# Gated mix of linear and local attention on one core: 14 instead of 9 matmuls on zeros at the start, and GpSimd's sums of phi(k) placed three at a time behind attention masks

## The chip, the cores and the metric

The kernel runs on one core of a Trainium2 chip. The metric is the device time of one execution in microseconds (us); lower is better. The kernel before took 491.21 us, the median of three runs (489.88, 491.21 and 491.37).

## The reference

For one sequence of 2048 positions x 1024 features, bf16, with 32 heads of 32, two attentions are computed on the same input `A_x` and mixed by a gate for each position:

```python
g = sigmoid((x * gate_w).sum(-1, keepdims=True))
# A: linear attention
phi = lambda t: where(t > 0, t + 1, exp(t)) + 1e-6
pq, pk = phi(q), phi(k)
kv = einsum("bhsd,bhse->bhde", pk, v)
z = einsum("bhsd->bhd", pk)
o = einsum("bhqd,bhde->bhqe", pq, kv) / (einsum("bhqd,bhd->bhq", pq, z)[..., None] + 1e-6)
a = o @ wo_A
# B: softmax over the 8 keys at distances 0, 2, ..., 14
b = softmax(q . k_gathered * scale) @ v_gathered @ wo_B
out = g * a + (1 - g) * b
```

Each of A and B has its own `wqkv` and `wo`. The change touches `z`, the sum of phi(k) over all positions, and the start of the program.

## The kernel before

**How the program is ordered.** The function `plan` records every operation with an engine, a cost, what it reads and writes, and a priority (by default the order of recording). A list scheduler (`Prog.schedule`, L121) turns this into one fixed order for each engine, and `Prog.emit` (L203) writes it out with semaphore waits. Each engine executes its own queue in order. `Prog.op` takes `after=`, a list of operations that the new one must wait for beside its data. Evictions from PSUM (`move`, L1367) are recorded for "any" of ScalarE and VectorE, and the scheduler picks one.

**The stages on TensorE (PE).**

1. At L1377 a loop of `WARM` (L1242, 9) matmuls on a tile of zeros, `warm`, runs ahead of all data. They write PSUM bank 7 and nobody reads it.
2. v of B (L1383): for blocks of four x tiles and two halves of the weight, 8 matmuls of 128x512 a group. The x tiles come by transposing DMAs from the queue of SyncE (SP in the profile) (`load_x`, L1311), the first weight half in four parts, two of them from ScalarE's queue. The first group (tile 0) is recorded in four steps of two matmuls, each waiting for its part of the weight. The results go to HBM (`vB_hbm`).
3. The gate, then k and q of B (L1502), 8 + 8 column blocks for each of the two halves of positions (even and odd).
4. phi(k) of A (L1546): 16 tiles x 2 halves, each 8 matmuls, then `phi` (L1347): an exponential on ScalarE, two VectorE operations, into `pkS`, all 16 tiles of which stay in SBUF.
5. x^T phi(k) (L1602, the matmuls L1610): 8 chunks x 2 halves, 16 matmuls each, then `state` (L1584) for kv.
6. phi(q) of A, the scaling by the denominators (`scaled`, L1648, which reads `zb`), and the output matmuls (L1678).

**The attention blocks of B.** `fill` (L1431) records one block: scores on PE (L1444), an exponential of all of them on ScalarE (`E`, L1450), a multiplication by a 0/1 mask on VectorE (L1453, the "mask"), and, three slots later, the products with the values on PE (`values`, L1456, matmuls L1463 and L1469), whose sums go through a logarithm and an exponential on ScalarE (L1478, L1479) and a product on VectorE (L1480). Scores and values share PSUM banks 4 to 7. There are 18 blocks; `slot` (L1488) spreads them among the matmul groups of stages 3 to 5.

**The sums.** z is made on GpSimd (POOL in the profile): a copy of tile 0 of `pkS` to the fp32 tile `zacc`, then 15 additions of a tile of 128x1024 (L1571 to L1576). The loop stands behind the one of stage 4, and the copy waits (`after=[o]`) for the last matmul group of phi(k). Behind chunks 5 and 6 of stage 5 `z_spread` (L1558) splits one half of `zacc` into two bf16 tiles (a cast L1560 into the tile `warm`, a subtraction L1561), multiplies both by ones on PE (L1566, the "z pair") to spread the sum to all partitions, and moves the result to `zb`.

Of the kernel before, what the change touches and what calls it, by code (L numbers as in the profile page):

```python
# [7 lines left out]
ALU = mybir.AluOpType  # L8
# [1103 lines left out]
def build_kernel(nc, A_x, A_wqkv, A_wo, B_x, B_wqkv, B_wo, gate_w, out):  # L1112
    del B_x
    S = A_x.shape[1]
    NT = S // 128
# [72 lines left out]
    pkS = SB([128, NT, 1024], BF16, "pk", at=ws[1].lo)  # L1188
# [15 lines left out]
    zacc = SB([128, 1024], F32, "zacc")  # L1204
# [34 lines left out]
    FILL = 0.2  # L1239
    PVLAG = 3  # L1240
    SUMS_AT = 2
    WARM = 9  # L1242
    PASSES = 6
    mm = lambda n: max(n / 2400.0, 0.0267) + 0.0025
    act = lambda n: 0.19 + n / 1200.0
# [2 lines left out]
    def plan(seen):  # L1248

        P = Prog(nc, nc.alloc_semaphore)  # L1250
# [27 lines left out]
        for i, (n, offs) in enumerate(KINDS):  # L1278
            for h, o in enumerate(offs):
                m = mtmp[h]  # L1280
# [102 lines left out]
        for t, half in [(4 * b + i, half) for b in range(NT // 4) for half in range(2) for i in range(4)]:  # L1383
# [5 lines left out]
            for d in range(0, 8, step):  # L1389
                o = group(bank, xs, w, [xr, ws[0].part((d, d + step), (half * 512, half * 512 + 512))], d, d + step)  # L1390
            move(vt[:, :], bank.ap, 512, bank, vt.all())
            P.op("sp", lambda e, t=t, vt=vt, half=half: e.dma_start(vB_hbm[t * 128:(t + 1) * 128, half * 512:half * 512 + 512], vt[:, :]), 0.6, reads=[vt.all()],
                 writes=[hb(t * 128, (t + 1) * 128, half)], chan="vst%d" % vs, lat=0.5, prio=5)
# [32 lines left out]
        main = Pool(banks[0:4])  # L1426
        todo = []
        later = []
        slot_n = [0]

        def fill(e_, qs, nq, offs):  # L1431
            t0 = e_ * HS
            k0 = [qs + nq * h - offs[h] for h in range(2)]
            m = msk[KINDS.index((nq, offs))]
            vt, vslot = vr.next()
            for h in range(2):
                P.op("sp", lambda e, h=h: e.dma_start(vt[64 * h:64 * h + 64, :], vB_hbm[t0 + k0[h]:t0 + k0[h] + 64, :]), 0.4,
                     reads=[hb(t0 + k0[h], t0 + k0[h] + 64, i) for i in range(2)], writes=[vt.all()], chan="v%d_%d" % (vslot, h), lat=0.5)

            def s_fn(e):  # L1440
                for c in range(8):
                    for h in range(2):
                        for j in range(4):
                            last = e.matmul(SO[j].ap(c * nq, (c + 1) * nq)[64 * h:64 * h + 64, :], kT[32 * j:32 * j + 32, c, t0 + k0[h]:t0 + k0[h] + 64],  # L1444
                                            qT[32 * j:32 * j + 32, c, t0 + qs + h * nq:t0 + qs + (h + 1) * nq], start=True, stop=True, tile_position=(32 * j, 64 * h))
                return last
            P.op("pe", s_fn, 0.65, mode="r", reads=[kT.part((0, 8), (t0 + k0[0], t0 + k0[1] + 64)), qT.part((0, 8), (t0 + qs, t0 + qs + 2 * nq))],
                 writes=[s.iv for s in SO], name="S")
            E, _ = Er.next()
            P.op("act", lambda e: e.activation(E[:, 0:32 * nq].rearrange("p (j q) -> p j q", j=4), ps[:, 4:8, 0:8 * nq], ACT.Exp), act(32 * nq),  # L1450
                 reads=[s.iv for s in SO], writes=[E.all()])
            ev = lambda: E[:, 0:32 * nq].rearrange("p (g q) -> p g q", g=16)
            P.op("dve", lambda e: e.tensor_tensor(ev(), ev(), m[:, :, :].rearrange("p r q -> p (r q)")[:, None, :].to_broadcast([128, 16, 2 * nq]), ALU.mult),  # L1453
                 0.15 + 32 * nq / 1920.0, reads=[E.all(), m.all()], writes=[E.all()])

            def values():  # L1456

                def each(e):
                    for c in range(8):
                        for j in range(4):  # L1460
                            for h in range(2):
                                hd = 4 * c + j
                                last = e.matmul(SO[h].ap(c * nq, (c + 1) * nq)[32 * j:32 * j + 32, :], vt[64 * h:64 * h + 64, hd * 32:hd * 32 + 32],  # L1463
                                         E[64 * h:64 * h + 64, (8 * j + c) * nq:(8 * j + c + 1) * nq],
                                         start=True, stop=True, tile_position=(64 * h, 32 * j))
                        if c == SUMS_AT:
                            for j in range(4):
                                for h in range(2):
                                    e.matmul(SO[2 + h].ap(0, 8 * nq)[32 * j:32 * j + 32, :], ones[64 * h:64 * h + 64, 0:32],  # L1469
                                             E[64 * h:64 * h + 64, 8 * j * nq:8 * (j + 1) * nq],  # L1470
                                             start=True, stop=True, tile_position=(64 * h, 32 * j))
                    return last
                bi = [s.iv for s in SO]
                P.op("pe", each, 0.66, mode="c", reads=[vt.all(), ones.all(), E.all()], writes=bi, name="PV")
                for g in range(2):
                    L, _ = Lr.next()
                    pb = lambda o, g=g: ps[:, 4 + 2 * o:6 + 2 * o, 4 * g * nq:4 * (g + 1) * nq]
                    P.op("act", lambda e, L=L, pb=pb: e.activation(L[:, :, 0:4 * nq], pb(1), ACT.Ln), act(8 * nq), reads=[SO[2].iv, SO[3].iv], writes=[L.all()])  # L1478
                    P.op("act", lambda e, L=L: e.activation(L[:, :, 0:4 * nq], L[:, :, 0:4 * nq], ACT.Exp, scale=-1.0), act(8 * nq), reads=[L.all()], writes=[L.all()])  # L1479
                    P.op("dve", lambda e, L=L, pb=pb, g=g: e.tensor_tensor(  # L1480
                        qT[:, 4 * g:4 * g + 4, t0 + qs:t0 + qs + 2 * nq].rearrange("p c (h q) -> p h c q", h=2),
                        pb(0).rearrange("p h (c q) -> p h c q", c=4), L[:, :, 0:4 * nq].rearrange("p h (c q) -> p h c q", c=4), ALU.mult), dps(8 * nq),
                        reads=[SO[0].iv, SO[1].iv, L.all()], writes=[qT.part((4 * g, 4 * g + 4), (t0 + qs, t0 + qs + 2 * nq))])
            after(PVLAG, values)
# [12 lines left out]
        def after(n, f, cols=False):  # L1497
            later.append((slot_n[0] + n, f, cols))
            later.sort(key=lambda x: x[0])
# [68 lines left out]
            P.op("pe", fn, 2 * mm(512), reads=[ones.all()] + [z.all() for z in zh], writes=[bank.iv], name="z")  # L1568
            move(zb[:, c], bank.ap, 512, bank, zb.part((hf * 512, (hf + 1) * 512)))

        for t in range(NT):  # L1571
            src = pkS.part((t, t + 1), (0, 1024))
            if t == 0:
                P.op("pool", lambda e: e.tensor_copy(zacc[:, :], pkS[:, 0, :]), 2.0, reads=[src], writes=[zacc.all()], after=[o])
            else:
                P.op("pool", lambda e, t=t: e.tensor_tensor(zacc[:, :], zacc[:, :], pkS[:, t, :], ALU.add), 2.2, reads=[src, zacc.all()], writes=[zacc.all()])  # L1576

        main = Pool(banks[0:3])
        sb = banks[3]
        sb.take = len(takes)  # L1580
# [3 lines left out]
        def state(c):  # L1584
            def fn(e):
                for i in range(8):
                    for j in range(4):
                        h = 4 * i + j
                        last = e.matmul(sb.ap()[32 * j:32 * j + 32, i * 32:i * 32 + 32], ws[0][:, c, h * 32:(h + 1) * 32], mT[:, c, h * 32:(h + 1) * 32],  # L1589
                                        start=False, stop=(c == 7), tile_position=(0, 32 * j), skip_group_check=True)  # L1590
                return last
            P.op("pe", fn, 0.22, mode="c", reads=[ws[0].part((c, c + 1), (0, 1024)), mT.part((c, c + 1), (0, 1024))], writes=[sb.iv], name="kv")
# [3 lines left out]
        def late_w():  # L1596
            if wait_w[0] and not todo:
                wait_w[0] = False
                load_w(5, 0, Ao, 0, 52)
                load_w(5, 1, Ao, 512, 53)  # L1600

        for c in range(8):  # L1602
            tl = xns[c // 2]
            cs = (c % 2) * 128
            for r in range(2):
                bank = main.next()
                for t0 in (0, NT // 2):
                    def fn(e, bank=bank, t0=t0, tl=tl, cs=cs, r=r):
                        for t in range(t0, t0 + NT // 2):
                            last = e.matmul(bank.ap(), tl[:, t, cs:cs + 128], pkS[:, t, r * 512:(r + 1) * 512], start=(t == 0), stop=(t == NT - 1))  # L1610
                        return last
                    P.op("pe", fn, NT // 2 * mm(512), reads=[tl.part((t0, t0 + NT // 2), (cs, cs + 128)), pkS.part((t0, t0 + NT // 2), (r * 512, (r + 1) * 512))], writes=[bank.iv])
                    if t0:
                        move(mT[:, c, r * 512:(r + 1) * 512], bank.ap, 512, bank, mT.part((c, c + 1), (r * 512, (r + 1) * 512)))
                    slot(FILL)
                    late_w()
            after(3, lambda c=c: state(c))
            if c in (5, 6):
                z_spread(c - 5)
            if c % 2 == 1 and len(xns) < 4:  # L1620
                xns.append(load_xn(len(xns)))
# [113 lines left out]
    P, flag_op = best[:2]  # L1735
# [61 lines left out]
```

## Time and profile before

| | |
|---|---|
| median of three runs | 491.21 us (489.88 to 491.37) |
| the profiled execution: its own time, its span | 491.46 us, 489.6 us |
| PE busy | 476.8 us, 97% |
| VectorE (DVE), ScalarE (ACT), GpSimd (POOL) busy | 277.6, 147.7, 44.2 us |
| phi(k) of A ends, stage 5 begins on PE | about 248.5 us |
| the sums on GpSimd (L1574, L1576) | 248.5 to 285.2 us |
| the attention masks L1453 | 18, from 132.4 to 312.1 us |

The profile is of one execution. Times in it are microseconds from the start of the span; the execution's own time is 1.86 us more than its span. A row of the timeline has the start, the duration, the engine, the line of the kernel, the operation, the tile written and the tiles read, the count of merged instructions, and in brackets how long the engine had been idle and what ended that. PEld is PE's weight load, which runs beside the matmuls. A row of the waits says who waited for whom: total us, times, longest. A row of one line has the shortest, median and longest duration in ns. A row of the DMA issues ends with the us from issue to landing. A row of the table of stretches has the busy us and count of PE, PEld, DVE, ACT and POOL, then the granted clock, the DMA share and GB/s.

### The profile page before, as it was taken

What the parts mean: (1) busy time and instruction counts of PE and PEld (TensorE: products, weight loads), DVE (VectorE), ACT (ScalarE), POOL (GpSimd) and SP (SyncE); (2) the same over time, 40 slices, a digit from 0 to 9 for tenths busy, and PEclk for the clock granted to TensorE, in tenths of its full rate; (3) what the DMA queues carried; (4) which work ended last, traced back from release to release, by engine and by line L of the source; (5) the groups of instructions that cost most, each with busy time, mean ns of one, the idle gap of its engine ahead of it and who ended that gap; (6) DMA issues with size and microseconds to landing.
All of it is one profiled execution on the core that took longest, in us unless ns stands there. A gap on an engine that the chain in (4) does not pass through costs nothing.

```text
span 489.6 us, 10831 instructions
## 1 busy us (share of the span) xinstructions
PE 476.8 (97%) x4815; PEld 226.8 (46%) x4878; DVE 277.6 (57%) x457; ACT 147.7 (30%) x229; POOL 44.2 (9%) x43
## 2 busy tenths in 40 slices
PE   8999999999999999999999999999999999999997
PEld 2444444444444444444445455444444444444444
DVE  2121235556577778776652323379987777777622
ACT  1211111111333335666644454545222100011000
POOL 3000000000000000000069941000000000000000
PEclk9999999999999999999999999999999999999999
DMA  8999996000000032303003340251224211123111
GB/s 212 230 190 279 355 308 168 0 1 0 1 25 23 24 108 66 36 23 120 23 25 110 120 121 3 90 172 23 64 66 107 44 43 44 44 57 73 44 44 48
DMA packets 72496, 43.27 MB, mean 88 GB/s; under 512 B 39157, under 2 KB 68214, under 8 KB 72442
## 3 DMA queue, kind: packets, MB, share of 16 engines
q1 hardware_dynamic: 71898, 41.98, 32.2%
q8 instruction: 40, 0.66, 0.6%
q10 hardware_dynamic: 544, 0.52, 0.4%
q14 instruction: 14, 0.11, 0.1%
HBM read 25.70 MB, written 8.40 MB: 70 GB/s over the span
## 4 chain that ended last, share of the span: by engine, by line
PE 96%; issue 2%; DMA 1%; DVE 1%; ACT 0%
PE ps_all L1343 56%; PE ps_all L1678 23%; PE ps_all L1610 10%; PE ps_all L1444 2%; PE ps_all L1463 2%; DMA xT<-in_A_x_dram 1%; PE ps_all L1469 1%; DVE E L1453 1%; PE ps_all L1589 0%; PE ps_all L1407 0%; ACT E L1450 0%; PE ps_all L1633 0%; PE ps_all L1566 0%; DVE o L1373 0%
## 5 line engine op out<-in xcount | busy, mean ns | idle before, releaser
L1343 PE MATMUL ps_all<-w,xT 128*128 128x512 bf16 x494 | 111.8, 384 | 3.1 <-issue 2.1
L1343 PE MATMUL ps_all<-xT,w 128*128 128x512 bf16 x497 | 109.9, 379 | 1.7 <-issue 1.4
L1343 PEld LDWEIGHTS ps_all<-w,xT 128*128 128x128 bf16 x512 | 49.5, 99 | 60.8 <-issue 4.4
L1343 PEld LDWEIGHTS ps_all<-xT,w 128*128 128x128 bf16 x512 | 49.3, 98 | 58.8 <-issue 0.4
L1349 ACT ACTIVATE e<-ps_all 128x512 bf16<-128x512 f32 x64 | 38.2, 598 | 111.9 <-PE ps_all L1343 110.1
L1678 PE MATMUL ps_all<-kT,aT 128*128 128x512 bf16 (+1 forms) x261 | 60.4, 373 | 0.2
L1678 PE MATMUL ps_all<-w,qT 128*128 128x512 bf16 (+1 forms) x259 | 60.2, 372 | 0.3
L1343 PE MATMUL ps_all<-kT,xT 128*128 128x512 bf16 x248 | 57.1, 379 | 0.6 <-issue 0.3
L1610 PE MATMUL ps_all<-pk,xn 128*128 128x512 bf16 x244 | 55.1, 379 | 1.8 <-issue 1.7
L1678 PEld LDWEIGHTS ps_all<-w,qT 128*128 128x128 bf16 x264 | 25.8, 98 | 29.7
L1678 PEld LDWEIGHTS ps_all<-kT,aT 128*128 128x128 bf16 x264 | 25.8, 98 | 29.4 <-issue 0.2
L1343 PEld LDWEIGHTS ps_all<-kT,xT 128*128 128x128 bf16 x256 | 24.7, 98 | 30.0 <-issue 0.5
L1610 PEld LDWEIGHTS ps_all<-pk,xn 128*128 128x128 bf16 x256 | 24.2, 98 | 27.8
L1370 DVE CAST vst<-ps_all 128x512 bf16<-128x512 f32 x15 | 10.4, 692 | 46.6 <-PE ps_all L1343 46.6
L1373 DVE TENSOR_SCALAR o<-ps_all,gm 128x512 bf16<-128x512 f32 (+1 forms) x27 | 19.7, 731 | 28.2 <-PE ps_all L1678 28.2
L1350 DVE TENSOR_SCALAR e<-e 128x512 bf16<-128x512 bf16 x64 | 18.5, 291 | 28.5 <-ACT e L1349 28.5
L1480 DVE TENSOR_TENSOR qT<-ps_all,L 128x456 bf16<-128x456 f32 (+1 forms) x36 | 21.1, 626 | 23.9 <-ACT L L1479 23.9
L1576 POOL TENSOR_TENSOR zacc<-zacc,pk 128x1024 f32<-128x1024 f32 x15 | 34.4, 2297 | 1.2
L1453 DVE TENSOR_TENSOR E<-E,msk 128x1824 bf16<-128x1824 bf16 (+1 forms) x18 | 22.5, 1250 | 21.1 <-ACT E L1450 21.1
L1450 ACT ACTIVATE E<-ps_all 128x1824 bf16<-128x1824 f32 (+1 forms) x18 | 30.4, 1688 | 12.4 <-PE ps_all L1444 11.5
L1370 DVE CAST kT<-ps_all 128x512 bf16<-128x512 f32 x25 | 17.1, 689 | 24.5 <-PE ps_all L1343 23.8
L1371 ACT ACTIVATE vst<-ps_all 128x512 bf16<-128x512 f32 x17 | 10.2, 597 | 49.2 <-PE ps_all L1343 49.2
(67 smaller groups left out, 336.0 us busy)
## 6 DMA issues: line engine op xcount, KB each, us to landing
v<-vB_hbm SPq DMA_DIRECT2D x36, 128.0 KB, 2.6
vB_hbm<-vst SPq DMA_DIRECT2D x32, 128.0 KB, 4.6
w<-in_B_wqkv_dram SPq DMA_DIRECT2D x4, 1024.0 KB, 8.2
xn<-in_A_x_dram SPq DMA_DIRECT2D x8, 512.0 KB, 6.4
w<-in_A_wqkv_dram SPq DMA_DIRECT2D x4, 1024.0 KB, 9.2
out_dram<-o SPq DMA_DIRECT2D x15, 256.0 KB, 2.1
kT<-in_A_wqkv_dram SPq DMA_DIRECT2D x2, 1024.0 KB, 5.9
kT<-in_A_wo_dram SPq DMA_DIRECT2D x2, 1024.0 KB, 5.6
```

What stands on the lines that cost most here:

```text
L1343: last = e.matmul(bank.ap(), lhs(dc), rhs(dc), start=(dc == 0), stop=(dc == 7))
L1349: P.op("act", lambda e: e.activation(e_[:, :], bank.ap(), ACT.Exp), act(512), reads=[bank.iv], writes=[e_.all()])
L1350: P.op("dve", lambda e: e.tensor_scalar(e_[:, :], e_[:, :], 1.0, 1e-6, op0=ALU.min, op1=ALU.add), 0.25, reads=[e_.all()], writes=[e_.all()])
L1370: fd = lambda e: e.tensor_copy(dst, src())
L1371: fa = lambda e: e.activation(dst, src(), ACT.Copy)
L1373: fd = lambda e: e.tensor_scalar(dst, src(), scale, None, op0=ALU.mult)
L1450: P.op("act", lambda e: e.activation(E[:, 0:32 * nq].rearrange("p (j q) -> p j q", j=4), ps[:, 4:8, 0:8 * nq], ACT.Exp), act(32 * nq), rea ...
L1453: P.op("dve", lambda e: e.tensor_tensor(ev(), ev(), m[:, :, :].rearrange("p r q -> p (r q)")[:, None, :].to_broadcast([128, 16, 2 * nq]), ...
L1480: P.op("dve", lambda e, L=L, pb=pb, g=g: e.tensor_tensor(qT[:, 4 * g:4 * g + 4, t0 + qs:t0 + qs + 2 * nq].rearrange("p c (h q) -> p h c q" ...
L1576: P.op("pool", lambda e, t=t: e.tensor_tensor(zacc[:, :], zacc[:, :], pkS[:, t, :], ALU.add), 2.2, reads=[src, zacc.all()], writes=[zacc.a ...
L1610: last = e.matmul(bank.ap(), tl[:, t, cs:cs + 128], pkS[:, t, r * 512:(r + 1) * 512], start=(t == 0), stop=(t == NT - 1))
L1678: last = e.matmul(bank.ap(0, f1 - f0), lh[:, k, t * 128:(t + 1) * 128], w[:, k, f0:f1], start=(first and k == 0), stop=(not first and k == 7))
```

## The change

Five more matmuls on zeros are recorded (14). The additions on GpSimd are no longer recorded in one loop: `z_add(n)` records the next n. Three (the copy and two additions) are recorded where the loop stood; three more follow each time a new attention block has been recorded in stage 5; what is left is recorded ahead of the spreads. Each is ordered behind the mask of the latest block recorded by then (`masks[-1:]`). The copy's cost in the planner goes from 2.0 to 1.2.

```diff
-    WARM = 9
+    WARM = 14
...
+        masks = []
...
-            P.op("dve", lambda e: e.tensor_tensor(ev(), ev(), m[:, :, :].rearrange("p r q -> p (r q)")[:, None, :].to_broadcast([128, 16, 2 * nq]), ALU.mult),
+            mk = P.op("dve", lambda e: e.tensor_tensor(ev(), ev(), m[:, :, :].rearrange("p r q -> p (r q)")[:, None, :].to_broadcast([128, 16, 2 * nq]), ALU.mult),
                  0.15 + 32 * nq / 1920.0, reads=[E.all(), m.all()], writes=[E.all()])
+            masks.append(mk)
...
-        for t in range(NT):
-            src = pkS.part((t, t + 1), (0, 1024))
-            if t == 0:
-                P.op("pool", lambda e: e.tensor_copy(zacc[:, :], pkS[:, 0, :]), 2.0, reads=[src], writes=[zacc.all()], after=[o])
-            else:
-                P.op("pool", lambda e, t=t: e.tensor_tensor(zacc[:, :], zacc[:, :], pkS[:, t, :], ALU.add), 2.2, reads=[src, zacc.all()], writes=[zacc.all()])
-
+        zadds = list(range(NT))
+
+        def z_add(n):
+            for t in zadds[:n]:
+                src = pkS.part((t, t + 1), (0, 1024))
+                if t == 0:
+                    P.op("pool", lambda e: e.tensor_copy(zacc[:, :], pkS[:, 0, :]), 1.2, reads=[src], writes=[zacc.all()], after=[o] + masks[-1:])
+                else:
+                    P.op("pool", lambda e, t=t: e.tensor_tensor(zacc[:, :], zacc[:, :], pkS[:, t, :], ALU.add), 2.2, reads=[src, zacc.all()], writes=[zacc.all()],
+                         after=masks[-1:])
+            del zadds[:n]
+
+        z_add(3)
+        n_masks = [len(masks)]
...
                     slot(FILL)
                     late_w()
+                    if len(masks) > n_masks[0]:
+                        n_masks[0] = len(masks)
+                        z_add(3)
             after(3, lambda c=c: state(c))
             if c in (5, 6):
+                z_add(NT)
                 z_spread(c - 5)
```

What this does to the order of each engine: PE, VectorE, GpSimd and SyncE keep their order but for the five zeros and the two z pairs. The first z pair now stands behind the scores of the last attention block, where the second stood; the second stands 16 matmuls of L1610 later, ahead of that block's values. The two evictions of z to `zb` move from VectorE to ScalarE: the first stands behind the exponential of the last block, the second ahead of that block's logarithms, with one eviction of stage 5 between them. On GpSimd the copy waits for the mask that starts at 254.35 us in the profile above; the third, sixth, ninth, twelfth and fifteenth additions wait for the next five masks in turn.

## The prediction

> **What bounds the kernel now.** First the page: its first lines, the chain of work that ended last, and the waits of PE.
>
> ```profile
> span 489.6 us, 10831 instructions
> PE 476.8 (97%) x4815; PEld 226.8 (46%) x4878; DVE 277.6 (57%) x457; ACT 147.7 (30%) x229; POOL 44.2 (9%) x43
> ...
> PE 96%; issue 2%; DMA 1%; DVE 1%; ACT 0%
> ```
> ```profile
> PE ps_all L1343 <- issue: 3.8, 24, 0.2
> PE ps_all L1610 <- issue: 1.7, 11, 0.2
> PE ps_all L1378 <- DVE warm L1291: 1.3, 1, 1.3
> PE ps_all L1463 <- DVE E L1453: 1.0, 1, 1.0
> PE ps_all L1343 <- DMA xT<-in_A_x_dram: 0.7, 1, 0.7
> ```
>
> TensorE bounds it: 476.8 of 489.6 us. It waits for another engine at three places only: the start (1.3), the first data (0.7), and once for an attention block's mask (1.0). So a change can gain at such a place, or where PE is busy but slow. The second kind is in the timeline of the first 30 us (start, duration; PEld is the weight load ahead of each matmul).
>
> ```profile
> 1.25 4.02 PE L1378 MATMUL ps_all<-warm 128*128 128x512 bf16 x9 [1.25 <-DVE warm L1291]
> ...
> 6.01 24.23 PE L1343 MATMUL ps_all<-w,xT 128*128 128x512 bf16 x100 [0.74 <-DMA xT<-in_A_x_dram]
> 6.39 0.15 PEld L1343 LDWEIGHTS ps_all<-w,xT 128*128 128x128 bf16 x1 [0.28 <-issue]
> ...
> 9.80 0.15 PEld L1343 LDWEIGHTS ps_all<-w,xT 128*128 128x128 bf16 x1 [0.28 <-issue]
> ...
> 10.22 19.74 PEld L1343 LDWEIGHTS ps_all<-w,xT 128*128 128x128 bf16 x92 [0.26 <-issue]
> ```
> ```profile
> 1.25:6.01 4.76, 4.02 (x9) 1.23 (x10) 2.23 (x8) 1.28 (x1) 3.74 (x17) 1.00 0.88 227
> 6.01:10.22 4.21, 4.21 (x11) 1.47 (x12) 0.00 (x0) 0.60 (x1) 0.00 (x0) 1.00 1.12 248
> ```
>
> From 6.39 to 9.80 there are eight steps of 0.426 us; from 10.22 on, 19.74/92 = 0.215. So the first ten real matmuls run at half pace and cost 10 x (0.426 - 0.215) = 2.11 us more than later ones. The clock column of the two stage rows (seventh, 1.00) does not show this; the spacing does. The nine matmuls on zeros (4.02 us, 1.25 to 5.27) were not followed by full pace: 0.74 us of idle lies behind them, and full pace came 4.21 us after 6.01.
>
> **Part 1, five more matmuls on zeros.** They add no data and no wait, and write a PSUM bank that the first stage leaves alone; the first real matmul stands behind them in PE's order. My reading: full pace comes after about 4.2 us of matmuls without a gap (4.02 was too little, 4.21 enough). From 1.25 that is ten zeros, to 1.25 + 10 x 0.426 = 5.51; the other four take 4 x 0.215, to 6.37. So real work starts 0.36 later than at 6.01 but at full pace. Its operands:
>
> ```profile
> 3.34 5.07 SPq L1313 DMA_TRANSPOSE xT<-in_A_x_dram  x3
> 4.62 3.79 SPq L1313 DMA_TRANSPOSE xT<-in_A_x_dram  x2
> 7.09 1.31 SPq L1313 DMA_TRANSPOSE xT<-in_A_x_dram  x1
> ```
> ```profile
> xT<-in_A_x_dram SPq DMA_TRANSPOSE x1, 4.9
> ...
> xT<-in_A_x_dram SPq DMA_TRANSPOSE x1, 4.6
> ...
> xT<-in_A_x_dram SPq DMA_TRANSPOSE x1, 3.5
> ```
>
> These are the loads of tiles 1, 2 and 3 of x, each timeline window opening with the next, and their times to landing, in the same order: 8.24, 9.22, 10.59. Tile 0's eight matmuls end at 6.37 + 8 x 0.215 = 8.09. Tile 1 lands 0.15 later; counting the 0.14 between tile 0's landing (0.80 + 5.07) and its first matmul, tile 1 starts at 8.38 and ends at 10.10. Tile 2 is wanted then and landed at 9.22; tile 3 is wanted at 11.82. Before, these sixteen matmuls ended at 6.01 + 10 x 0.426 + 6 x 0.215 = 11.56. Gain: 11.56 - 10.10 = **1.46 us**, kept to the end because PE waits for nothing that the profile names until the mask, 240 us later. No earlier release of the clock gives more: tile 1's landing is the floor. If instead all fourteen run at half pace (to 1.25 + 14 x 0.426 = 7.21) and full pace comes just then, the sixteen end at 10.65 and the gain is 0.91.
>
> The Trainium skill's page "TensorE: Matmul & The Clock Gate", section "What's actually happening", says that the clock is released by a busy window of 3413 ns that runs freely, whatever the kernel does; an estimate by it is a gain between 0.5 us and the floor's, changing from run to run. The half pace ahead of 10.22 agrees; that the place changes no single trace can show.
>
> **Part 2, GpSimd's sums.** In the kernel before, the copy and fifteen adds follow each other; they meet the masks.
>
> ```profile
> 249.66 35.55 POOL L1576 TENSOR_TENSOR zacc<-zacc,pk 128x1024 f32<-128x1024 f32 x15
> ```
> ```profile
> L1453 DVE TENSOR_TENSOR E<-E,msk x18: 1093/1108/2815, 132.4 to 312.1; 128x1824 bf16<-128x1824 bf16 x16, 128x1792 bf16<-128x1792 bf16 x2
> ```
> ```profile
> L1576 POOL TENSOR_TENSOR zacc<-zacc,pk x15: 2125/2130/3056, 249.7 to 283.1; 128x1024 f32<-128x1024 f32 x15
> ```
> ```profile
> 252.83 3.40 PE L1610 MATMUL ps_all<-pk,xn 128*128 128x512 bf16 x15
> ...
> 254.35 2.81 DVE L1453 TENSOR_TENSOR E<-E,msk 128x1824 bf16<-128x1824 bf16 x1 [3.90 <-ACT E L1450]
> ...
> 257.22 0.28 PE L1463 MATMUL ps_all<-E,v 64*32 64x57 bf16 x24 [0.99 <-DVE E L1453]
> ```
>
> The mask at 254.35 took 2.81 against a median of 1.11, while adds ran. PE had ended at 252.83 + 3.40 = 256.23 and waited 0.99. In the changed program the copy waits for this very mask, so nothing of GpSimd's runs beside it: it ends at 255.46, 0.77 ahead of PE's need. What is late next is PE itself. Gain: **0.99 us**.
>
> What the move puts at risk: GpSimd's queue is in order, so every later add stands behind the wait of the first of its three. The later masks:
>
> ```profile
> 265.74 1.11 DVE L1453 TENSOR_TENSOR E<-E,msk 128x1824 bf16<-128x1824 bf16 x1 [4.96 <-ACT E L1450]
> ...
> 275.51 1.10 DVE L1453 TENSOR_TENSOR E<-E,msk 128x1824 bf16<-128x1824 bf16 x1
> ...
> 285.33 1.52 DVE L1453 TENSOR_TENSOR E<-E,msk 128x1824 bf16<-128x1824 bf16 x1 [3.54 <-ACT E L1450]
> ...
> 294.11 1.11 DVE L1453 TENSOR_TENSOR E<-E,msk 128x1824 bf16<-128x1824 bf16 x1 [3.54 <-ACT E L1450]
> ...
> 302.89 1.62 DVE L1453 TENSOR_TENSOR E<-E,msk 128x1824 bf16<-128x1824 bf16 x1 [0.53 <-ACT E L1450]
> ```
>
> Masks start 8.78 to 9.82 apart. Take an add at 2.2 with its gap: three take 6.6, and with the mask's 1.11 that is 7.7, so each three ends about 1.1 ahead of the next mask. The chain: copy and two adds behind the first mask, threes behind the next four, the fifteenth add behind the one at 302.89. Then the spreads:
>
> ```profile
> 301.70 0.61 POOL L1560 CAST warm<-zacc 128x512 bf16<-128x512 f32 x1 [13.84 <-PE ps_all L1566]
> 302.39 1.16 POOL L1561 TENSOR_TENSOR zl<-zacc,warm 128x512 bf16<-128x512 f32 x1
> ```
> ```profile
> 310.46 0.38 PE L1566 MATMUL ps_all<-zl,ones 128*128 128x512 bf16 x1 [0.16 <-issue]
> 310.68 3.62 PE L1610 MATMUL ps_all<-pk,xn 128*128 128x512 bf16 x16
> ```
>
> On the old times less the 0.99: the last mask of the chain ends near 302.6 (it also comes 0.38 earlier, since the first z pair no longer precedes it), the last add at 304.9, cast and subtraction by 307.0. The first z pair now stands on PE where the second stood, 310.46 - 0.99 - 0.38 = 309.1: 2.1 us of slack. The second pair goes sixteen matmuls further, at about 312.9, and its operands follow the first pair by 0.61 + 1.16, by 311.4: 1.5 of slack. The number of PE instructions on z is the same, so the move itself is worth 0. The two evictions of z go from DVE to ScalarE; one stands ahead of a logarithm that PE does not wait for. I take 0, with 0.6, one such eviction (the next row), as the upper bound.
>
> ```profile
> 314.33 0.60 ACT L1371 ACTIVATE mT<-ps_all 128x512 bf16<-128x512 f32 x1 [2.29 <-PE ps_all L1610]
> ```
>
> **Sum.** The profiled execution took 491.46 us with a span of 489.6. 491.46 - 1.46 - 0.99 = **489.0 us**. It lies 0.25 above the median of the three runs, 491.21; they spread from 489.88 to 491.37. The lowest is 1.58 below the profiled one, about what an early release is worth here (1.46), so the pace may already come earlier in some runs before. That makes the gain against a median uncertain, hardly the time itself, which has the floor.
>
> **Rivals.**
> A. The release follows a beat of its own instead of 4.2 us without a gap. Then the gain of part 1 lies between 0.49 (two real matmuls still slow behind 7.21: 0.91 - 2 x 0.211) and 1.46. For it: the spread of the runs. Time: 489.0 to 490.0, the middle 489.5.
> B. Only one part works: the clock gains but a mask still waits as at 254.35, or the reverse. The point is an add of (8.78 - 1.11)/3 = 2.56; the longest add row is 3.06, the median 2.13. Beyond it a three meets the next mask, whose price is about the 0.99 already seen: 490.0 with one, 491.0 with two. Against it: two of three masks met by adds before (265.74, 275.51) were not stretched. The reverse, no gain of the clock, gives 490.5.
> C. Slower: matmuls on zeros do nothing for the clock, which then answers only to real matmuls. The rows allow it: the nine were followed by half pace. Real work starts at 7.21 instead of 6.01 and pays the same ten slow matmuls: 491.46 + 1.20 - 0.99 = 491.7; if it falls half such a stretch later still, five more slow matmuls (5 x 0.211) make it 492.8. It decides if the spacing stays 0.426 past 10.22. Against it: the low run of 489.88 had nothing else visible to gain 1.5 us from.
> D. The chain of sums ends after 309.1 and PE waits for z; it needs 2.1 us of delay. 1 us late beyond that gives 490.0.
>
> **How the numbers follow.** Forecast 489.0 (488.6 to 489.4): 0.52. A: 0.22. B: 0.15. C: 0.08. D and the rest: 0.03. A difference of about 0.3% (1.5 us) is what a measurement of this kernel tells from none; below 489.7 counts as faster. Faster: the forecast and most of A, 0.68; same: the rest of A, B, D and half of C, 0.28; slower: half of C, 0.04. The range goes from 488.5 to 490.6: it holds the forecast, all of A and most of B and D.
>
> **What would show it.** Part 1: the weight loads of zeros change from 0.426 to about 0.215 apart near 5.5 us, all real ones are about 0.215 apart, and a short wait for tile 1 of x stands at 8.1 to 8.4. Slow real matmuls behind 7.2 speak for A, ten or more for C. Part 2: all masks at about 1.1, adds in threes with idle between them that a mask ends, no PE wait for L1453's successor, the first z pair starting without a wait. The prediction is wrong if the first real matmul starts at 7.2 and stays slow, or if PE waits for GpSimd at z.

## The result, and the profile after

The changed kernel took **489.25 us**, the median of 11 runs (488.87 to 489.77). The kernel before, in 11 runs, took 490.21 us (489.69 to 491.4). The ratio is 0.9978, with a 95% interval from 0.9968 to 0.9988: 0.22% faster, or about 1 us. The three runs known when the prediction was made had a median of 491.21; eight more brought it down to 490.21. The spread of the kernel before is 1.7 us, more than the whole effect, so a single execution of each says little.

The two profiled executions lie at opposite ends of these spreads: the changed one took 488.87 us (span 487.0), the lowest of its runs, and the one before 491.46, above the highest of its eleven. They differ by 2.59 us. First the page of the changed one.

```profile
span 487.0 us, 10907 instructions
...
PE 98%; DMA 1%; SPq 0%; DVE 0%; issue 0%
```

Then PE's waits for other engines (total us, times, longest). The row for the mask is gone, and that for x is down from 0.7 to 0.2.

```profile
PE ps_all L1378 <- DVE warm L1291: 1.3, 1, 1.3
PE ps_all L1343 <- DMA xT<-in_A_x_dram: 0.2, 1, 0.2
```

Where the 2.59 us went is read from the chain of work that ended last, which is nearly all PE. These are its rows for the gate (L1407), the first row of stage 5 (L1619, formerly L1610) and the last eviction (L1373).

```profile
61.82 1.84 PE ps_all L1407 x32
...
246.76 3.45 PE ps_all L1619 x16
...
484.22 0.48 DVE o L1373
```

In the chain before, the same three began at 63.48, 248.47 and 487.00.

```profile
63.48 1.84 PE ps_all L1407 x32
...
248.47 3.45 PE ps_all L1610 x16
...
487.00 0.48 DVE o L1373
```

So in this pair 1.66 us were won ahead of the gate, 0.05 more up to stage 5, and 1.07 between there and the last eviction; 0.19 of these 2.78 were lost again behind it. In size these are the two terms of the sum, 1.46 and 0.99. The second is the mask, as the timeline of VectorE and PE after shows:

```profile
252.64 1.11 DVE L1454 TENSOR_TENSOR E<-E,msk 128x1824 bf16<-128x1824 bf16 x1 [4.04 <-ACT E L1451]
```
```profile
250.90 3.62 PE L1619 MATMUL ps_all<-pk,xn 128*128 128x512 bf16 x16
254.45 0.28 PE L1465 MATMUL ps_all<-E,v 64*32 64x57 bf16 x24
```

The mask takes 1.11 instead of 2.81 and ends at 253.75, 0.70 ahead of the products with the values, which follow the matmuls without a gap. The first is in PE's weight loads of the first 9 us:

```profile
3.79 0.15 PEld L1378 LDWEIGHTS ps_all<-warm 128*128 128x128 bf16 x1 [0.28 <-issue]
4.22 1.21 PEld L1378 LDWEIGHTS ps_all<-warm 128*128 128x128 bf16 x6 [0.28 <-issue]
5.79 0.55 PEld L1343 LDWEIGHTS ps_all<-w,xT 128*128 128x128 bf16 x4 [0.36 <-DMA xT<-in_A_x_dram]
...
8.06 5.95 PEld L1343 LDWEIGHTS ps_all<-w,xT 128*128 128x128 bf16 x29 [0.68 <-DMA xT<-in_A_x_dram]
```

The six zeros from 4.22 on stand about 0.2 apart, no longer 0.426: full pace came while PE still worked on zeros, some 3 us after 1.25. About half of the fourteen zeros were slow and half fast, and every real matmul is fast. Tile 1 of x is waited for until 8.06. But in the profile before, the nine zeros ran for 4.02 us and none of them got full pace. A stretch of 3 us in one run and not of 4 us in another: the place of the release is not fixed by the kernel. That speaks for the prediction's rival A, by which the 1.66 us belong to these two executions and not to the change; the experiments test it.

### The profile page after: what moved, and what is told of

The parts are those of the page before. It is cut to its first block, busy times and chain, and to the rows that moved or that the text cites. A ratio compares the mean times of both kernels' runs of the same rounds, so it can differ in the third digit from the quotient of the medians.

```text
span 487.0 us, 10907 instructions
## 1 busy us (share of the span) xinstructions
PE 482.7 (99%) x4883; PEld 226.3 (46%) x4883; DVE 273.7 (56%) x455; ACT 148.6 (31%) x231; POOL 40.9 (8%) x43
## 4 chain that ended last, share of the span: by engine, by line
PE 98%; DMA 1%; SPq 0%; DVE 0%; issue 0%
PE ps_all L1343 57%; PE ps_all L1691 23%; PE ps_all L1619 12%; PE ps_all L1445 2%; PE ps_all L1465 2%; DMA xT<-in_A_x_dram 1%; PE ps_all L1471 1%; PE ps_all L1598 1%; PE ps_all L1407 0%; PE ps_all L1646 0%; SPq L1313 0%; SPq L1318 0%; PE ps_all L1568 0%; DVE o L1373 0%; PE ps_all L1591 0%
## 5 line engine op out<-in xcount | busy, mean ns | idle before, releaser
L1343 PE MATMUL ps_all<-w,xT 128*128 128x512 bf16 x512 | 113.3, 379 | 0.2 <-DMA xT<-in_A_x_dram 0.2
L1343 PE MATMUL ps_all<-xT,w 128*128 128x512 bf16 x512 | 112.2, 379 | 0.0
L1619 PE MATMUL ps_all<-pk,xn 128*128 128x512 bf16 x256 | 57.8, 379 | 0.0
L1619 PEld LDWEIGHTS ps_all<-pk,xn 128*128 128x128 bf16 x256 | 24.1, 98 | 27.6
L1454 DVE TENSOR_TENSOR E<-E,msk 128x1824 bf16<-128x1824 bf16 (+1 forms) x18 | 20.4, 1133 | 27.3 <-ACT E L1451 27.3
L1373 DVE TENSOR_SCALAR o<-ps_all,gm 128x512 bf16<-128x512 f32 (+1 forms) x27 | 19.7, 730 | 28.2 <-PE ps_all L1691 28.2
L1581 POOL TENSOR_TENSOR zacc<-zacc,pk 128x1024 f32<-128x1024 f32 x15 | 31.9, 2130 | 16.6 <-DVE E L1454 15.8
L1371 ACT ACTIVATE kT<-ps_all 128x512 bf16<-128x512 f32 x23 | 13.2, 597 | 38.4 <-PE ps_all L1343 36.9
```

The source lines that it names most:

```text
L1343: last = e.matmul(bank.ap(), lhs(dc), rhs(dc), start=(dc == 0), stop=(dc == 7))
L1371: fa = lambda e: e.activation(dst, src(), ACT.Copy)
L1373: fd = lambda e: e.tensor_scalar(dst, src(), scale, None, op0=ALU.mult)
L1454: mk = P.op("dve", lambda e: e.tensor_tensor(ev(), ev(), m[:, :, :].rearrange("p r q -> p (r q)")[:, None, :].to_broadcast([128, 16, 2 * n ...
```

## The experiments

**Theory after the result.** Full pace is released at a beat of its own, at another place in every run, after a stretch nearly filled with matmuls. The nine zeros of the kernel before already get it in many runs. So the five more zeros save nothing in those, and about 1.5 us in the others, while in some runs they put the first real matmul off. The moved sums save 1.0 us in every run. **Rivals:** the recorded reading (4.2 us without a gap, so a fixed gain); zeros that do nothing; for the sums, that the spacing in threes is what gains.

**One part each.** `zeros14_only` is the kernel before with one edit, `sums_only` the changed kernel with one edit:

```diff
-    WARM = 9
+    WARM = 14
```
```diff
-    WARM = 14
+    WARM = 9
```

> The kernel before with 14 matmuls on zeros, its sums as they were. Theory (a beat of its own: full pace comes at a place that changes from run to run, after a stretch that is nearly filled with matmuls, and in about half of the runs of the kernel before it comes already during the nine zeros): the median is about 490.2, close to that of the kernel before, but the runs near 491.3 are gone: lowest about 489.8, highest about 490.8. Rival 1 (the recorded reading: 4.2 us without a gap): full pace always at 5.5, all runs within 0.3 of 490.0, and the kernel before always near 491.4. Rival 2 (the zeros do nothing): as the kernel before, runs from 489.7 to 491.4.

Measured: 490.36 us (490.0 to 490.81, 11 runs); the kernel before, 490.37 (489.69 to 492.37, 33 runs). Ratio 0.9995, interval 0.9985 to 1.0005.

> The changed kernel with 9 matmuls on zeros, so only the sums are moved. Theory: every run is 1.0 less than a run of the kernel before with the same release: median about 489.2, runs from 488.7 to 490.4, and the profile shows no wait of PE for a mask. If the zeros made the gain (rival): median about 490.2. If both parts add as the prediction had it: 490.2, 1.5 above the changed kernel's runs of early release.

Measured: 489.29 us (488.76 to 490.39, 12 runs), ratio 0.9978, interval 0.9966 to 0.9990.

The zeros alone change nothing that can be measured in the median; they cut off the top of the spread, as expected (no run above 490.81), and its bottom too (490.0 against 489.69). In the mean they gain 0.25 us (490.37 against 490.62). The sums alone give the whole gain of the changed kernel. Four of their twelve runs lie between 490.05 and 490.39, about 1 us above the rest: by the theory the nine zeros missed the release there, which no profile of those four shows.

The profile of `sums_only` is of one of the other runs (489.14). It has the same nine zeros as the kernel before. Here are its rows of PE, and the gate in its chain:

```profile
1.25 3.62 PE L1378 MATMUL ps_all<-warm 128*128 128x512 bf16 x9 [1.25 <-DVE warm L1291]
5.94 2.15 PE L1343 MATMUL ps_all<-w,xT 128*128 128x512 bf16 x8 [1.07 <-DMA xT<-in_A_x_dram]
```
```profile
61.97 1.84 PE ps_all L1407 x32
```

The first eight real matmuls take 2.15 us; at half pace they would take 8 x 0.426 = 3.41. So with nine zeros full pace was there for the first data in this execution, and not in the profile before. The gate begins at 61.97 instead of 63.48, only 0.15 behind the changed kernel's 61.82: nearly all of the 1.66 us comes without the five zeros.

The sums' part, in contrast, hardly changes from profile to profile. From the start of stage 5 to the last eviction the chain takes 238.53 us in both profiles with the old order (`zeros14_only`: 247.32 to 485.85) and 237.35 to 237.48 in all six with the threes.

The profile of `zeros14_only` shows the release at yet another place, in PE's weight loads:

```profile
1.25 0.13 PEld L1378 LDWEIGHTS ps_all<-warm 128*128 128x128 bf16 x2 [1.25 <-DVE warm L1291]
...
6.35 0.15 PEld L1378 LDWEIGHTS ps_all<-warm 128*128 128x128 bf16 x1 [0.28 <-issue]
6.75 8.30 PEld L1343 LDWEIGHTS ps_all<-w,xT 128*128 128x128 bf16 x39 [0.25 <-issue]
```

Here PE worked on zeros for 5.5 us without a gap at half pace. That rules out the recorded reading (4.2 us). And it shows the price: the first real weights load behind all fourteen zeros, at 6.75 instead of the 5.79 of the changed kernel's profile.

**How many zeros.** `zeros11` is the changed kernel with 11, `zeros20` with 20 (their cost for the planner scaled, so that all else keeps its order):

```diff
-    WARM = 14
+    WARM = 11
```
```diff
-    WARM = 14
+    WARM = 20
...
-            P.op("pe", lambda e: e.matmul(banks[7].ap(), warm[:, 0:128], warm[:, :], start=True, stop=True), 0.43, reads=[warm.all()], writes=[banks[7].iv], prio=-1)
+            P.op("pe", lambda e: e.matmul(banks[7].ap(), warm[:, 0:128], warm[:, :], start=True, stop=True), 0.301, reads=[warm.all()], writes=[banks[7].iv], prio=-1)
```

> The changed kernel with 11 matmuls on zeros, which at half pace end at 1.25 + 11 x 0.426 = 5.94, just where the first data comes. Theory (beat): the gap that spoils a release is closed and no real matmul is put off, so median about 488.9 and a spread of about 0.4 instead of 0.9. Rival 1 (4.2 us without a gap): 488.9 too, spread 0.1. Rival 2 (zeros do nothing): 489.25, spread as before.

Measured: 488.97 us (488.6 to 489.19, 9 runs), ratio 0.9965, interval 0.9952 to 0.9978.

> The changed kernel with 20 matmuls on zeros, the same order of all else. Theory (beat): six more zeros put the first real matmul off by 6 x 0.215 = 1.3 at least, of which the wait for tile 1 of x takes up to 0.2: median about 490.4, runs from 489.7 to 491.3. Rival 1 (4.2 us without a gap): 7.66 as the start of real work in every run, 490.1, spread 0.1. Rival 2 (zeros do nothing at all, PE's start is hidden): 489.25.

Measured: 490.15 us (489.54 to 490.9, 11 runs), ratio 0.9995, interval 0.9986 to 1.0004.

Both came near to what the theory had. The median of the twenty is nearer to the recorded reading's 490.1 than to the theory's 490.4; what speaks against that reading is the spread, 1.36 us instead of 0.1. Not all of that spread need come from the start: in the profiled execution, the highest, PE also stood still once for 0.6 us at 201.06, for no cause that the profile names. Eleven at half pace end just where the data comes, so they close the gap and put hardly anything off. Twenty give back all that the sums gained; if zeros did nothing at the start, they would have cost nothing. `zeros11` was run again as the base of the next set:

> The kernel with 11 matmuls on zeros and the moved sums once more, as the base of the three other kernels of this set, which all have 11 zeros. Theory (beat): again 488.9 to 489.1 with a spread of 0.6 at most, and full pace at another place between 4.2 and 8 us in the profile. Rival (the small spread before was chance): some of eleven runs above 489.6.

Measured: 489.19 us (488.58 to 489.54, 10 runs), ratio 0.9975, interval 0.9965 to 0.9985. No run lies above 489.6. The two medians of one kernel, 488.97 and 489.19, show what a median of ten is worth here. In both profiles the release came near 4.2, so this run did not show the other place that was expected of it; where two more kernels used the same eleven zeros it came near 4.9 (`sums_one_go`) and 7.2 (`sums_by_four`). This is the row of the latter:

```profile
6.77 0.15 PEld L1343 LDWEIGHTS ps_all<-w,xT 128*128 128x128 bf16 x1 [0.28 <-issue]
7.15 0.75 PEld L1343 LDWEIGHTS ps_all<-w,xT 128*128 128x128 bf16 x4 [0.23 <-issue]
```

So the place moves by some 3 us between executions whose start is the same. It is not all that moves: with the release near 4.2 in both, the first real matmul began at 5.77 in `zeros11` and at 6.22 in `zeros11_again`, since its data came later, and the gate at 61.77 and 62.22. That is 0.45 of the 0.58 us between these two executions (488.6 and 489.18).

**What in the sums' move gains.** `sums_one_go` lets only the copy wait, for the first mask, and all fifteen additions follow; `sums_by_four` takes four behind each mask. Both have 11 zeros. In both the z pairs also stand where they stood in the kernel before, and VectorE makes the two evictions to `zb` again.

```diff
-        z_add(3)
+        z_add(NT)
         n_masks = [len(masks)]
```
```diff
-        z_add(3)
+        z_add(4)
         n_masks = [len(masks)]
...
-                        z_add(3)
+                        z_add(4)
```

> 11 zeros; copy and all fifteen additions behind the first mask alone, with no wait for the later masks. Theory 1 (the whole 1.0 us of the sums' move is the one stretched mask; later masks that meet additions have slack on PE): the first mask at 1.11, one or more of the next three masks stretched by up to 2.1, PE waits for at most one of them, 0 to 1.4 us in all; median 489.0 to 489.9. Rival (a mask that meets the additions always waits for the one in flight and PE with it, so the threes are what gains): three masks stretched, PE waits 2 to 3 us, 491.

Measured: 488.85 us (488.72 to 489.42, 8 runs), ratio 0.9971, interval 0.9959 to 0.9982; the median is a little below the 489.0 to 489.9 expected. These are its masks from the timeline of VectorE:

```profile
252.73 1.11 DVE L1454 TENSOR_TENSOR E<-E,msk 128x1824 bf16<-128x1824 bf16 x1 [4.04 <-ACT E L1451]
263.04 1.70 DVE L1454 TENSOR_TENSOR E<-E,msk 128x1824 bf16<-128x1824 bf16 x1 [4.96 <-ACT E L1451]
272.81 1.50 DVE L1454 TENSOR_TENSOR E<-E,msk 128x1824 bf16<-128x1824 bf16 x1
282.63 1.26 DVE L1454 TENSOR_TENSOR E<-E,msk 128x1824 bf16<-128x1824 bf16 x1 [3.54 <-ACT E L1451]
291.41 1.76 DVE L1454 TENSOR_TENSOR E<-E,msk 128x1824 bf16<-128x1824 bf16 x1 [3.54 <-ACT E L1451]
300.32 1.62 DVE L1454 TENSOR_TENSOR E<-E,msk 128x1824 bf16<-128x1824 bf16 x1 [0.53 <-ACT E L1451]
```

Three masks meet additions, and the last two meet the two subtractions of the spreads; all five are stretched. The list of PE's waits names none of them. The threes are not needed here: what gains is that the first mask is out of the additions' way. That the other masks cost so little is in part luck. The one at 291.41 was stretched by 0.65, and PE's products with the values began 1.82 after its start instead of 1.70 (in the changed kernel 293.02 after 291.32): 0.12 late, which is also what the chain from stage 5 to the last eviction is longer by (237.59).

> 11 zeros; the additions four at a time behind a mask. A four takes 8.7 us against 8.66, 8.7 and 7.67 between the end of one mask and the start of the next. Theory: only the last of these is clearly too short; that mask is stretched by about 1.05 to 2.16, PE has 0.65 in hand and waits 0.4; median 489.0 to 489.5. Rival (the prediction's B: each collision costs about 1.0, for two or three masks): 490 to 492.

Measured: 489.27 us (489.07 to 490.08, 12 runs), ratio 0.9980, interval 0.9972 to 0.9989. The mask behind the last four is the only one that the additions stretch, and PE waits 0.4 for it, as was expected. The wait of PE, the mask, and the addition in flight as that mask starts, each from its view:

```profile
PE ps_all L1465 <- DVE E L1454: 0.4, 1, 0.4
```
```profile
290.50 2.12 POOL L1581 TENSOR_TENSOR zacc<-zacc,pk 128x1024 f32<-128x1024 f32 x1
...
291.46 2.12 DVE L1454 TENSOR_TENSOR E<-E,msk 128x1824 bf16<-128x1824 bf16 x1 [3.54 <-ACT E L1451]
```

The addition ends 1.16 after the mask's start, and the mask takes 1.01 more than its 1.11. The kernel before has the same picture at its two ends. This is its timeline at 254.35 and at 275.51:

```profile
254.08 2.12 POOL L1576 TENSOR_TENSOR zacc<-zacc,pk 128x1024 f32<-128x1024 f32 x1
```
```profile
275.54 3.06 POOL L1576 TENSOR_TENSOR zacc<-zacc,pk 128x1024 f32<-128x1024 f32 x1
```

At 254.35 the addition had 1.85 to go, and the mask took 1.70 more. At 275.51 the mask was 0.03 us earlier than the addition, and the addition took 0.93 more. In these rows the later one waits for the earlier one as a whole. The Trainium skill's page "SBUF — State Buffer", section "Who interferes with whom", says that a VectorE instruction with two SBUF inputs contends with a GpSimd instruction that reads SBUF, and that such contention is an exclusive lock; all these rows agree.

**The floor of the start.** `w_on_act` (11 zeros) moves two weight loads from SyncE's queue to ScalarE's, so that tile 1 of x is issued earlier. The planner also reorders some evictions and later loads in it.

```diff
-        load_w(0, 0, Bw, 2048, 0.3, 4, 6)
-        load_w(0, 0, Bw, 2048, 0.4, 6, 8)
+        load_w(0, 0, Bw, 2048, 0.3, 4, 6, "act")
+        load_w(0, 0, Bw, 2048, 0.4, 6, 8, "act")
```

> 11 zeros; the third and fourth part of the first weight half are issued by ScalarE's queue behind the first two, so SyncE's queue goes from tile 0 of x straight to tile 1. Theory (the floor of the start is when tile 1 of x lands, and that hangs on when it is issued): tile 1 is issued at 2.2 instead of 3.33 and lands near 7.0, its first matmul starts at 7.5 instead of 8.07, median 488.4. Rival (the DMA engines are full in these microseconds, and the landing moves little): tile 0 or the weight parts land later by as much, and the median stays at 488.9 to 489.1 or rises.

Measured: 490.96 us (490.31 to 493.55, 12 runs), ratio 1.0019, interval 1.0005 to 1.0033: slower than the kernel before, and 1.77 us behind the eleven zeros of the same set (489.19). The theory had 488.4; it failed. The row of tile 1 of x among the DMA issues (stretch from 2.2 to 2.3 us) ends with its us to landing; then come PE's wait and its weight loads.

```profile
xT<-in_A_x_dram SPq DMA_TRANSPOSE x1, 7.2
```
```profile
PE ps_all L1343 <- DMA w<-in_B_wqkv_dram: 1.1, 1, 1.1
```
```profile
9.20 0.11 PEld L1343 LDWEIGHTS ps_all<-w,xT 128*128 128x128 bf16 x2 [1.58 <-DMA w<-in_B_wqkv_dram]
9.46 5.46 PEld L1343 LDWEIGHTS ps_all<-w,xT 128*128 128x128 bf16 x26 [0.15 <-DMA xT<-in_A_x_dram]
```

Tile 1 was issued 1.1 us earlier and landed at about 9.4, over 1 us later than before, and the last weight part was late too. An earlier issue did not bring an earlier landing here. In the profiled execution, the lowest of the twelve, the loss lies ahead of the gate: it begins at 63.34 instead of 62.22 in `zeros11_again`, and the times are 490.31 and 489.18. That the transfers share full DMA engines fits (the DMA share from 4 to 8 us is 1.15, and 1.13 in `zeros11_again`), but was not measured by itself; what the planner's other moves cost in the slower runs was not tried either.

## Why the prediction was right and wrong

The time lies in the range (488.5 to 490.6) and 0.25 us above the forecast of 489.0. The sign is right. The size of the gain is not: about 1 us, where the sum had 2.45, and the likeliest class (faster by over 0.3%, 0.68) did not come. That the time is right says little for the mechanism of part 1. It was taken down to the floor of the start, and an early release ends at that floor by whatever rule it comes; the range was drawn to hold rival A as well.

- **Part 2, the mask: right**, with its price. 0.99 was forecast; `sums_only` against the kernel before is 490.37 - 489.29 = 1.08, and the chains differ by 1.07. The first mask's 1.11, the threes of 6.55 and the z pairs without a wait came as described. One sign did not: not all masks stayed at 1.1. The last, at 308.86, met the second subtraction and took 1.63; PE did not wait for it. Moving z cost nothing.
- **Part 1, the zeros: the step that failed** is "full pace comes after about 4.2 us of matmuls without a gap", with a gain "kept to the end". Rival A came, its chance 0.22, as far as it says that the place changes from run to run; that the release keeps a regular beat is not shown. `zeros14_only` stayed at half pace for 5.5 us without a gap, and the changed kernel left it after 3. Alone the zeros are worth 490.37 - 490.36 = 0.01 us in the median instead of 1.46 (by the interval, between a gain of 0.7 and a loss of 0.25). By the theory, which is argued from the spreads, two things cancel: runs in which nine zeros miss the release gain, and runs in which fourteen slow zeros end behind the first data (7.21 against 6.01) lose part of it.
- **The base.** The sum was made against one execution of 491.46, whose release was late. The prediction saw that the low run of 489.88 fitted an early release, but went on to take late ones as the rule. In the 33 runs of the kernel before that stand beside `zeros14_only`, only nine lie above 491.0 and 19 below 490.5; in the 29 beside `w_on_act`, six and 23.
- **The floor: right in its nature.** In the profile after, tile 1 is waited for until 8.06 (8.38 was forecast), and fast matmuls follow each other without a gap from there. Moving the issue forward did not lower it.
- **Rivals C and D: out.** Zeros do release the clock (4.22 after), and the second spread had ended 1.4 us ahead of its z pair (308.39 + 1.16 against 310.92, from these two rows of the timeline after):

```profile
308.39 1.16 POOL L1563 TENSOR_TENSOR zl<-zacc,warm 128x512 bf16<-128x512 f32 x1
...
310.92 0.38 PE L1568 MATMUL ps_all<-warm,ones 128*128 128x512 bf16 x1
```

- **Rival B's price: smaller than 0.99.** The mask waits for the rest of the addition in flight, at most 2.1, and PE has some time in hand: in the changed kernel's timeline the first six masks of stage 5 end 0.59 to 1.64 ahead of PE's products. In `sums_one_go` five stretched masks cost PE about 0.1, in `sums_by_four` one cost 0.4. The argument that two masks "were not stretched" was also misread: one met the very end of an addition, the other won by 0.03 us.

The lowest medians are those with 11 zeros: 488.97 and 489.19 in two sets, and 488.85 with the additions in one go. Their ratios to the kernel before (0.9965, 0.9975, 0.9971) have intervals that overlap with the changed kernel's (0.9968 to 0.9988), so none is shown to be better than it.

## What to carry to other kernels

Before a gain is worked out from one execution, compare the spread of the known runs with the term: a spread as large as the term may be the term, present in some runs already. Matmuls on zeros ahead of the first data should end, at half pace, about where the data comes; many more of them move the real work (490.15 with twenty against 489.25 with fourteen). When VectorE and GpSimd meet, look for the one instruction whose stretch PE feels, and let just that one go first.

## What the runs showed of the hardware

- The place at which full matmul pace begins moved between 4.1 and 10.2 us over these executions. With eleven zeros alone it moved between 4.1 and 7.2. Zeros count for it: in the changed kernel it came at 4.22, when PE had worked on nothing else. In the profile before, full pace came only at 10.22, after 0.74 us of idle behind the nine zeros; that this idle held it up is not shown, and `sums_only` had 1.07 us of idle there and full pace behind it. The granted clock in the profile's rows stayed at 1.00 throughout; only the spacing of the weight loads (0.426 against 0.215) shows it.
- In these traces a VectorE product of two SBUF tiles and a GpSimd addition exclude each other for a whole instruction: the mask's extra time was the rest of the addition less about 0.15 (1.70 of 1.85, 1.01 of 1.16).
- The transposing load of tile 1 landed 4.7 us after its issue at 3.33 in the changed kernel, and 7.2 us after its issue at 2.2 where four weight loads had been issued from the other queue by 2.9 us.
